# One group of half-tile checks moved behind five row checks, and three weight loads moved behind two row loads, in a Fourier-mixing and one-token FFN kernel

## The chip, the core and the metric

The kernel runs on one core of one Trainium2 chip. The metric is the device time of one execution in microseconds. Three timed runs of the kernel before gave 203.41, 270.83 and 200.82 us; their median is 203.41 us. The execution that was profiled took 201.27 us.

A core has five engines that run side by side, each with its own instruction stream in fixed order: TensorE (PE, matrix products), VectorE (DVE), ScalarE (ACT), GpSimd (POOL) and SyncE (SP). An instruction that waits holds up everything behind it on its engine. Transfers between device memory and the on-chip buffer are issued by SP (ordinary loads, called direct) and by POOL (loads by a table of row numbers, called gathers); all of them share 16 DMA engines.

## The reference

The input `x` is 2048 tokens by 576 columns. The kernel computes a Fourier mixing layer with a residual, then a feed-forward network that runs for a single token:

```python
a = einsum("bsd,ed->bse", LN(x), dft_hid_re)          # 576 x 576
b = einsum("bsd,ed->bse", LN(x), dft_hid_im)
h = x + einsum("ts,bse->bte", dft_seq_re, a) - einsum("ts,bse->bte", dft_seq_im, b)   # 2048 x 2048
z = LN(h)
r = z @ w_r                                           # one score per token
t = argmax(r)                                         # C = 1: one token
y = (silu(z[t] @ w_gate) * (z[t] @ w_up)) @ w_down    # 576 -> 4608 -> 576
out = h + z;  out[t] += sigmoid(r[t]) * y
```

All data is float32. The four Fourier matrices and the three weight matrices come as inputs, and their bytes are most of what is read: 72.86 MB read and 6.49 MB written by the page.

## The kernel before

**What is computed quickly, and what is checked.** The sequence matrices are really cosines and sines, so one half of them is a mirror image of the other. The kernel multiplies with a quarter of each matrix only (lines 556 to 568) and, beside that, loads the rest as well and checks that it is the mirror image. The checks write differences (or sums) to a buffer `Q` on DVE; ACT squares `Q` and sums the squares (line 368). If the sum over all checks is not tiny at the end, a slow general path under `tc.If` computes everything anew (from line 1331). In the runs here it is not taken.

**How the sequence matrices are tiled.** There are 16 blocks of rows, `j` = 0 to 15, each for the cosine (`i` = 0) and the sine (`i` = 1). Blocks `j` and `16 - j` mirror each other. Group 0 of `GROUPS` is the blocks 1 to 5, called group one in the heading of this change; group 1 is 6, 7, 0, 8. For a group, the five (or four) block tiles of 128 x 1152 floats stay in a buffer `D` while PE multiplies with them: `D0` holds the cosine of the first group, `D1` its sine. These ten tiles are loaded by `c_first(0, 0)` and `c_first(0, 1)`, ahead of everything else of the matrices.

**The two kinds of check.**

- A half check (`off_h`, line 382): for tiles that PE uses, the second half of the 128 columns must mirror the first. It reads the tiles in `D` alone and needs no further load. One call is two DVE instructions (line 387).
- A row check (`c_check`, line 833): for block `j` it loads the mirrored part of `j` (a gather on POOL), block `16 - j` (a direct load on SP) and the mirrored part of `16 - j` (another gather); three DVE instructions compare them: line 375 twice (`off_s`) and line 380 once (`off_t`).

The loads of a row check go to a ring of buffers: seven called `R`, and those of the tiles in `D` that are free at the time. A load can be issued only when the checks that read its buffer before have run. In the first group the row check of block 1 uses `R` 0 to 2, that of block 2 `R` 3 to 5, that of block 3 `R` 6 and two tiles of `D2`; block 4 takes the other two tiles of `D2` and then `R` 0, block 5 `R` 2, 1 and 3. The first direct loads of the sine's row checks go to `R` 4 (freed by block 2) and `R` 2 (freed by the first instruction of block 5's cosine check); behind these two, in SP's order, stand the four tiles of the second group's cosine.

**The buffer Q** has two slots, taken in turn. A check that takes a slot waits for the square of the check that had it before.

**The weights W** of the hidden transform (`wt`, three tiles, four direct loads, lines 403 and 405) are needed by ACT (line 415) and then by PE (line 610), when all five products with the sequence matrix of the first group are done (`seq`, line 565) and written to `Z` by DVE (line 583).

**The order of the work.** The kernel is not written in order of time. A planner (`Plan`) gets every step with its engine, an estimated duration and what it depends on, and arranges the steps of each engine by a list schedule. The steps of SP and POOL that load are chained in the order in which the code makes them; on DVE and ACT the planner chooses among the steps that are ready. The order that comes out is fixed in the program: it is not changed at run time.

**What follows** the two groups: residual and row statistics on DVE and ACT, the choice of the token, and the feed-forward network, whose 31.9 MB of weights (three matrices of 576 x 4608 floats) are loaded into every buffer that comes free (lines 1173 to 1181) and multiplied on DVE, POOL and ACT; PE adds up the last product (line 1228), DVE finishes the token's row (line 1241), and it is stored.

Of the kernel before, what the change touches and what calls it, by code (L numbers as in the profile page):

```python
# [14 lines left out]
P = 128  # L15
# [22 lines left out]
GROUPS = [[1, 2, 3, 4, 5], [6, 7, 0, 8]]  # L38
# [5 lines left out]
HALVES = [[(0, 2), (2, 2), (4, 1)], [(0, 2), (2, 2)]]  # L44
# [8 lines left out]
HM = P // 2  # L53
# [17 lines left out]
class Plan:  # L71
# [6 lines left out]
    def add(self, eng, dur, fn, *deps, tail=0.0, push=0.0):  # L78
        flat = []
        for d in deps:  # L80
            flat += d if isinstance(d, list) else [d]
        n = {"eng": eng, "dur": dur, "fn": fn, "deps": [d for d in flat if d], "tail": tail, "push": push}
        n["i"] = len(self.ops)
        self.ops.append(n)
        return n
# [57 lines left out]
def kernel(  # L143
# [172 lines left out]
    Q = QT.bitcast(BF16).rearrange("p (n w) -> p n w", n=2)  # L316
# [62 lines left out]
        o = Q[:, u % 2, 14 * P : QW].rearrange("p (k m) -> p k m", m=P)  # L379
        dve.tensor_tensor(o, C[NK - j, i, False], C[j, i, False][:, :, ::-1], op=SIGN[i])  # L380

    def off_h(g, c, n, i, u):

        o = Q[:, u % 2, i * 9 * n * HM : (i + 1) * 9 * n * HM].rearrange("p (c k m) -> p c k m", k=9, m=HM)
        t = DT[g, i][:, c : c + n]
        for k, op in enumerate((OP.subtract, OP.add)):
            dve.tensor_tensor(o[:, :, k::2, :], t[:, :, k::2, 0:HM], t[:, :, k::2, HM:P], op=op)  # L387
# [296 lines left out]
    add = plan.add  # L684

    def then(f, *args):
        return lambda: f(*args)
# [8 lines left out]
    def load(eng, f, mb, *deps):  # L696

        ns = in_flight[eng]
        n = add(eng, 0.1 if eng == "SP" else 1.3, f, *deps, ns[-8:-7])
        d = add("DMA", mb / 0.405, None, n, moved[-1:])  # L700
        moved.append(d)
        ns.append(add("COME", 0.0, None, d, tail=1.8))
        return n, ns[-1]
# [4 lines left out]
    def in_turn(eng, f, mb, *deps):  # L708
        LAST[eng], d = load(eng, f, mb, LAST[eng], *deps)
        return d  # L710

    IDENT = []
    for k, n in X_LOADS:
        d = in_turn("SP" if k < 9 else "POOL", then(load_x, k, n), 0.295 * n)
# [11 lines left out]
    for a, b in X_RUNS:  # L726
# [4 lines left out]
        m = [add("ACT", 0.95, then(measure, k), f, push=push) for k, f in zip(ks, r)]  # L731
        o = add("POOL", 0.3, then(totals, a, b), e, m)
# [3 lines left out]
        o = add("POOL", 2.0, then(biases, a, b), r, o)  # L736
# [6 lines left out]
    users = {b: [] for b in ["XF", "Z", "Q", "WA", "WB", "WC", *range(N_RAW)]}  # L743
# [16 lines left out]
    for k in FOLDED:  # L760
        dg, use, at = [], [], []
        for sl in slots_of(k):
            n = next(places)
            UF[sl] = LATER[n]
            at.append(PLACE[n])
            if k in PAIRS:
                u, w = dgs.take()
# [34 lines left out]
    CU = {}  # L802

    def c_load(j, i, mirror):
        CU[j, i, mirror] = ring("POOL" if mirror else "SP", load_c, 0.46 if mirror else 0.59, j, i, mirror)
# [8 lines left out]
            LAST["SP"], d = load("SP", then(load_c, None, j, i, False), 0.59, w, LAST["SP"])  # L814
            CU[j, i, False] = u, d

    def c_half(g, c, m):
        u, w = qs.take()
        cus = [[CU[j, i, False] for j in GROUPS[g][c : c + m]] for i in range(2)]
        n = [  # L820
            add("DVE", 0.16 + 0.62 * m, then(off_h, g, c, m, i, u), [d for _, d in cus[i]], w)
            for i in range(2)
        ]
        for i in range(2):
            for b, _ in cus[i]:
                users[b].append(n[i])
        squares(u, 9 * m * P, n)

    def squares(u, w, n, ps=P):
        SQUARES.append(add("ACT", 0.3 + w / 1200, then(square, u, w, ps), n))  # L830
        qs.users[u].append(SQUARES[-1])

    def c_check(j, i):

        u, w = qs.take()
        u0, d0 = CU[j, i, False]
        c_load(j, i, True)
        u1, d1 = CU[j, i, True]
        n = [add("DVE", 1.08, then(off_s, j, i, u, 0), d0, d1, w)]
        users[u0] += n  # L840
        users[u1] += n
        free.append(u1)
        if j in PAIRS:
            m = NK - j
            c_load(m, i, False)
            c_load(m, i, True)
            (u2, d2), (u3, d3) = CU[m, i, False], CU[m, i, True]
            n.append(add("DVE", 1.08, then(off_s, m, i, u, 1), d2, d3, w))
            users[u3].append(n[1])
            n.append(add("DVE", 1.36, then(off_t, j, i, u), d0, d2, w))  # L850
            users[u0].append(n[2])
            users[u2] += n[1:]
            free.extend([u3, u2])
        if u0[0] == "D1":
            free.append(u0)
        squares(u, QW if j in PAIRS else 7 * P, n)
# [3 lines left out]
    def w_first():  # L860
        for n in range(3):
            LAST["SP"], d = load(
                "SP", then(load_w, None, n), (0.59, 0.59, 0.22)[n], LAST["SP"], users["W" + "ABC"[n]]
            )
            WL.append(d)
# [19 lines left out]
    def seq_step(g, n):  # L885
        nonlocal pe_last
        w = len(GROUPS[g]) * HM
        (z0, w0_), (z1, w1_) = zs.take(), zs.take()
        need = [CU[j, i, False][1] for i in PARTS[n] for j in GROUPS[g]]
        pe_last = add("PE", 9 * w * 0.00171, then(seq, g, n), need, FOLDS, w0_, w1_, pe_last)  # L890
        for i in PARTS[n]:
            for c in range(len(GROUPS[g])):
                users[D_TAG[g, i], c].append(pe_last)
        users["XF"] = [pe_last]
        SEQ[g, n] = pe_last, z0, z1

    def keep_step(g, n):
        w = len(GROUPS[g]) * HM
        pe, z0, z1 = SEQ[g, n]
        u, wo = odds.take()  # L900
        h = add("ACT", 0.11 + 0.00085 * w, then(keep, g, n, 0), pe, wo)
        l = add("DVE", 2 * (0.07 + 0.00106 * w), then(keep, g, n, 1), h, ZU.get((g - 1, n > 0), []))
        odds.users[u].append(l)
        zs.users[z0].append(l)
        zs.users[z1].append(h)
        KEPT.setdefault(g, []).append(l)
# [44 lines left out]
        for b in [b for b in free if type(b) is tuple and b[0] == tag]:  # L951
            free.remove(b)

    for c, m in HALVES[0]:
        c_half(0, c, m)
    for j in GROUPS[0][:3]:
        c_check(j, 0)
    w_first()
    for j in GROUPS[0][3:]:
        c_check(j, 0)  # L960
    for n in (0, 1, 4, 2, 3):
        seq_step(0, n)
        keep_step(0, n)
# [18 lines left out]
    for i in range(2):  # L982
        for j in GROUPS[1]:
            c_check(j, i)
    for c, m in HALVES[1]:
        c_half(1, c, m)
    for c in range(2):
        hid_step(0, c)
    for n in (0, 1):
# [133 lines left out]
    o = add("DVE", 1.0, check_sum, SCORES, SQUARES, xs_is)  # L1123
    o = add("PE", 0.3, check_all, o)
# [6 lines left out]
    for b in range(NJ // TW):  # L1131
        j = TW * b
# [198 lines left out]
    with tc.If(T["mv"], preferred_fallthrough_block=False):  # L1331
        with ExitStack() as gen:
# [33 lines left out]
            with ExitStack() as hs:  # L1366
# [9 lines left out]
                with tc.For_i(0, NK, 1) as k:  # L1376
                    dve.tensor_copy(xr, row_of(GX, k))
                    norm(xn, xr, "x")
                    for a in range(5):
                        w = min(P, D - a * P)  # L1380
# [4 lines left out]
                    for c in range(4):  # L1385
                        pa = zbank(f"gpa{c}")
                        for a in range(5):
                            w = min(P, D - a * P)
# [115 lines left out]
```

## Time and profile before

| what | value |
|---|---|
| timed runs | 200.82, 203.41, 270.83 us (median 203.41) |
| profiled execution | 201.27 us, span from first to last instruction 199.2 us |
| busy: PE, DVE, ACT, POOL | 65%, 83%, 71%, 62% of the span |
| DMA | 77.81 MB moved, 391 GB/s over the span |

The page cuts the span into 40 slices of 5 us and gives, for each, how busy every engine was in tenths, and how many GB/s the DMA engines moved. Other views list the instructions of one engine in order of time; a row there gives start, duration, engine, line, operation, what is written and read, a count, and in brackets how long the engine had stood idle before it and what released it. Rows of `SPq` are the moments at which SP issues loads; a time there is the issue, not the transfer. A view of stretches gives the DMA's share and rate for any piece of time.

### The profile page before, as it was taken

How to read it: one execution, taken by the hardware profiler on the slowest of the kernel's cores; microseconds unless marked ns; L12 is line 12 of the kernel's file. 1: busy time of each engine (PE TensorE's matmuls, PEld its weight loads, DVE VectorE, ACT ScalarE, POOL GpSimd, SP SyncE). 2: the span in 40 equal slices, each digit the busy share in tenths (PEclk: the TensorE clock that was granted, in tenths of full speed). 3: DMA queues.
4: the chain of work that ended last, by engine and by line, in shares of the span. 5: the costliest groups of instructions: out<-in, count | busy, mean ns of one | idle time of the engine just before them, and what ended most of it. 6: DMA issues, size and time to landing. Idle time of an engine off the chain costs nothing. (4 is left out here: it accounts for less than half of the span.)

```text
span 199.2 us, 2787 instructions
## 1 busy us (share of the span) xinstructions
PE 130.4 (65%) x758; PEld 89.9 (45%) x758; DVE 166.1 (83%) x419; ACT 140.5 (71%) x259; POOL 122.8 (62%) x134
## 2 busy tenths in 40 slices
PE   0007989999999989899999996600241444085840
PEld 0005667764767778677877774400121111043220
DVE  4389997989999859997999999999839997899410
ACT  2298863783987794799587599997629999786400
POOL 6578888495528878998870000006439999998500
PEclk9999999999999999999999999985555555555798
DMA  5999999999979999999999999999999999999991
GB/s 190 361 418 415 411 411 409 409 372 346 402 275 366 415 398 391 404 407 412 407 401 418 420 420 422 427 414 423 422 428 425 428 422 420 431 420 412 422 387 42
DMA packets 14491, 77.81 MB, mean 391 GB/s; under 512 B 1855, under 2 KB 1859, under 8 KB 11143
## 3 DMA queue, kind: packets, MB, share of 16 engines
q1 hardware_dynamic: 10463, 56.56, 70.8%
q0 software_dynamic: 4000, 21.03, 26.3%
q8 instruction: 7, 0.11, 0.2%
q14 instruction: 13, 0.11, 0.1%
q10 hardware_dynamic: 8, 0.00, 0.0%
HBM read 72.86 MB, written 6.49 MB: 398 GB/s over the span
## 5 line engine op out<-in xcount | busy, mean ns | idle before, releaser
L368 ACT ACTIVATE Q<-Q 128x2944 bf16<-128x2944 bf16 (+5 forms) x26 | 55.4, 2133 | 19.9 <-DVE Q L375 7.0
L610 PE MATMUL py<-W,Z 128*128 128x289 f32 x180 | 45.3, 408 | 2.3 <-DVE X L619 2.3
L565 PE MATMUL ps<-D,XF 128*128 128x320 f32 (+3 forms) x216 | 45.0, 408 | 1.2 <-DMA D<-in_ct_dram 0.8
L301 POOL DMA_INDIRECT R<-in_ct_dram,ic x21 | 34.1, 1625 | 14.5 <-DVE Q L375 10.5
L610 PEld LDWEIGHTS py<-W,Z 128*128 128x128 f32 x180 | 33.7, 189 | 13.6 <-issue 2.9
L565 PEld LDWEIGHTS ps<-D,XF 128*128 128x128 f32 (+1 forms) x216 | 32.1, 172 | 13.8 <-issue 2.5
L1201 POOL TENSOR_TENSOR D<-D,Z 128x1152 f32<-128x1152 f32 x8 | 20.8, 2618 | 1.2 <-SPq L1331 1.2
L667 POOL DMA_DIRECT2D out_dram<-X x1 | 0.6, 606 | 30.0 <-ACT X L661 30.0
L301 POOL DMA_INDIRECT D<-in_ct_dram,ic x11 | 16.1, 1468 | 3.4 <-issue 2.4
L498 ACT ACTIVATE junk<-X,XT 128x576 bf16<-128x576 f32 x16 | 12.4, 772 | 8.0 <-DVE W L459 6.5
L1206 ACT ACTIVATE junk<-D 128x576 bf16<-128x576 f32 x20 | 13.7, 683 | 4.0 <-POOLq L1331 2.3
L1228 PE MATMUL pd<-XF,H 128*1 128x144 f32 x80 | 5.3, 440 | 16.1 <-DVE H L1220 13.3
L537 PE MATMUL fo<-W,diag 128*128 128x288 f32 (+1 forms) x8 | 3.9, 665 | 16.4 <-DVE diag L528 16.4
L387 DVE TENSOR_TENSOR Q<-D 128x640 bf16<-128x640 f32 (+3 forms) x20 | 12.7, 691 | 1.4 <-DMA D<-in_ct_dram 1.4
L380 DVE TENSOR_TENSOR Q<-R,D 128x1152 bf16<-128x1152 f32 x10 | 13.4, 1349 | 0.0
L630 ACT ACTIVATE junk<-X,TD 128x576 bf16<-128x576 f32 x16 | 12.3, 768 | 1.5 <-DVE X L619 1.3
L375 DVE TENSOR_TENSOR Q<-R,D 128x896 bf16<-128x896 f32 x11 | 11.9, 1083 | 1.3 <-DMA D<-in_ct_dram 1.2
L661 ACT ACTIVATE X<-X,BB,UP 128x576 f32<-128x576 f32 x14 | 10.8, 855 | 2.4 <-DVE BB L642 2.4
L623 DVE SCALAR_TENSOR_TENSOR junk<-X,wr 128x576 bf16<-128x576 f32 x16 | 12.1, 754 | 0.3
L375 DVE TENSOR_TENSOR Q<-D 128x896 bf16<-128x896 f32 x11 | 11.8, 1081 | 0.0
L619 DVE SCALAR_TENSOR_TENSOR X<-py,X 128x576 f32<-128x576 f32 x16 | 11.5, 748 | 0.0
L375 DVE TENSOR_TENSOR Q<-R 128x896 bf16<-128x896 f32 x10 | 10.8, 1084 | 0.7 <-DMA R<-in_ct_dram,ic 0.7
(202 smaller groups left out, 262.5 us busy)
## 6 DMA issues: line engine op xcount, KB each, us to landing
D<-in_ct_dram SPq DMA_DIRECT2D x22, 576.0 KB
R<-in_ct_dram SPq DMA_DIRECT2D x10, 576.0 KB
D<-in_wu_dram SPq DMA_DIRECT2D x5, 1152.0 KB
D<-in_wd_dram SPq DMA_DIRECT2D x4, 1152.0 KB
R<-in_wg_dram SPq DMA_DIRECT2D x3, 1152.0 KB
D<-in_wg_dram SPq DMA_DIRECT2D x3, 1152.0 KB
out_dram<-X SPq DMA_DIRECT2D x2, 1440.0 KB
X<-in_x_dram SPq DMA_DIRECT2D x4, 576.0 KB
```

What stands on the lines that cost most here:

```text
L301: pool.indirect_dma_start(tile, None, view, bass.IndirectOffsetOnAxis(ap=rows, axis=0), element_offset=at)
L368: act.activation(t, t, AF.Square, accum_out=DS[0 : t.shape[0], n : n + 1])
L375: dve.tensor_tensor(o, C[j, i, True][:, 0:7, :], C[j, i, False][:, 7:0:-1, :], op=SIGN[i])
L380: dve.tensor_tensor(o, C[NK - j, i, False], C[j, i, False][:, :, ::-1], op=SIGN[i])
L387: dve.tensor_tensor(o[:, :, k::2, :], t[:, :, k::2, 0:HM], t[:, :, k::2, HM:P], op=op)
L498: act.activation(junk[:, 0:D], X[:, k, 0:D], AF.Square, bias=XT[:, n : n + 1], scale=-float(D), accum_out=VX[:, n : n + 1],)
L565: pe.matmul(cm(ZP[g, n][k % 2][p0 : p0 + m], w), XF[:, q, m0 : m0 + m], DT[g, i][:, :, k, 0:HM], start=k in (0, 1), stop=k in (6, 7),)
L610: pe.matmul(YP[GROUPS[g][c]][:, h, 0:w], Z[:, a, c * P : (c + 1) * P], w_block(a)[:, h * HD : h * HD + w], start=(a == 0), stop=(a == 4),)
L623: dve.scalar_tensor_tensor(junk2, X[:, k, 0:D], 1.0, wr, op0=OP.mult, op1=OP.mult, accum_out=TD[:, n, 0:1])
L630: act.activation(junk[:, 0:D], X[:, k, 0:D], AF.Square, bias=TD[:, n, 1:2], scale=-float(D), accum_out=VAR[:, n : n + 1],)
L1201: pool.tensor_tensor(t, t, xs.unsqueeze(1).to_broadcast([P, JW, D]), op=OP.mult)
L1206: act.activation(junk[:, 0:D], WB[w, j][:, r, :], AF.Copy, accum_out=acc[:, j + r : j + r + 1])
```

## The change

`c_half` took one part of a group's tiles and compared its cosine and its sine together, one slot of `Q` for both. `halves` takes a list of parts and a list of cosine and sine. For the first group the cosine's halves of all five tiles now share one slot and stay where they were; the sine's halves share another slot and are made behind the five cosine row checks. The three tiles of W are loaded behind the loads of the fifth row check instead of behind those of the third. The second group is treated as before.

```diff
-    def off_h(g, c, n, i, u):
-
-        o = Q[:, u % 2, i * 9 * n * HM : (i + 1) * 9 * n * HM].rearrange("p (c k m) -> p c k m", k=9, m=HM)
+    def off_h(g, c, n, i, u, at):
+
+        o = Q[:, u % 2, at : at + 9 * n * HM].rearrange("p (c k m) -> p c k m", k=9, m=HM)
...
-    def c_half(g, c, m):
+    def halves(g, parts, ms):
         u, w = qs.take()
-        cus = [[CU[j, i, False] for j in GROUPS[g][c : c + m]] for i in range(2)]
-        n = [
-            add("DVE", 0.16 + 0.62 * m, then(off_h, g, c, m, i, u), [d for _, d in cus[i]], w)
-            for i in range(2)
-        ]
-        for i in range(2):
-            for b, _ in cus[i]:
-                users[b].append(n[i])
-        squares(u, 9 * m * P, n)
+        n, at = [], 0
+        for i in ms:
+            for c, m in parts:
+                cus = [CU[j, i, False] for j in GROUPS[g][c : c + m]]
+                o = add("DVE", 0.16 + 0.62 * m, then(off_h, g, c, m, i, u, at), [d for _, d in cus], w)
+                for b, _ in cus:
+                    users[b].append(o)
+                n.append(o)
+                at += 9 * m * HM
+        squares(u, at, n)
...
-    for c, m in HALVES[0]:
-        c_half(0, c, m)
+    halves(0, HALVES[0], [0])
     for j in GROUPS[0][:3]:
         c_check(j, 0)
-    w_first()
     for j in GROUPS[0][3:]:
         c_check(j, 0)
+    w_first()
+    halves(0, HALVES[0], [1])
...
-    for c, m in HALVES[1]:
-        c_half(1, c, m)
+    for part in HALVES[1]:
+        halves(1, [part], [0, 1])
```

What the planner makes of it. SP, the direct loads behind those of the ten tiles, before:

```order
L357 DMA R<-in_ct_dram 128x1152 x2
L357 DMA D<-in_ct_dram 128x1152
L403 DMA W<-in_wt_dram 128x2x576 x2
L403 DMA W<-in_wt_dram 33x2x576
L405 DMA W<-in_wt_dram 32x576
L357 DMA D<-in_ct_dram 128x1152
L357 DMA R<-in_ct_dram 128x1152 x3
L357 DMA D<-in_ct_dram 128x1152 x5
```

and now:

```order
L357 DMA R<-in_ct_dram 128x1152 x2
L357 DMA D<-in_ct_dram 128x1152 x2
L357 DMA R<-in_ct_dram 128x1152
L403 DMA W<-in_wt_dram 128x2x576 x2
L403 DMA W<-in_wt_dram 33x2x576
L405 DMA W<-in_wt_dram 32x576
L357 DMA R<-in_ct_dram 128x1152 x2
L357 DMA D<-in_ct_dram 128x1152 x5
```

The loads of blocks 12 (`D`) and 11 (`R`) have moved ahead of the four loads of W; all else on SP stands as before, and POOL's order is the same throughout.

DVE at the start of the checks, from the last fold of the input on, before (half checks of two parts, the first row check, half checks of the last two parts; the two parts ahead of these rows are the cosine and the sine of tiles 3 and 4):

```order
L548 TENSOR_SCALAR XF<-fo_370 128x287
L387 TENSOR_TENSOR Q<-D 128x2x5x64
L387 TENSOR_TENSOR Q<-D 128x2x4x64
L387 TENSOR_TENSOR Q<-D 128x2x5x64
L387 TENSOR_TENSOR Q<-D 128x2x4x64
L375 TENSOR_TENSOR Q<-R,D 128x896
L375 TENSOR_TENSOR Q<-R 128x896
L380 TENSOR_TENSOR Q<-R,D 128x1152
L387 TENSOR_TENSOR Q<-D 128x5x64
L387 TENSOR_TENSOR Q<-D 128x4x64
L387 TENSOR_TENSOR Q<-D 128x5x64
L387 TENSOR_TENSOR Q<-D 128x4x64
```

and now, at the same place:

```order
L548 TENSOR_SCALAR XF<-fo_370 128x287
L375 TENSOR_TENSOR Q<-R,D 128x896
L387 TENSOR_TENSOR Q<-D 128x5x64
L387 TENSOR_TENSOR Q<-D 128x4x64
L375 TENSOR_TENSOR Q<-R 128x896
L380 TENSOR_TENSOR Q<-R,D 128x1152
L724 TENSOR_SCALAR bt<-tf 128x16
L375 TENSOR_TENSOR Q<-R,D 128x896
L380 TENSOR_TENSOR Q<-R,D 128x1152
L375 TENSOR_TENSOR Q<-R 128x896
```

The first row check now begins behind two parts of the half checks (both cosine) instead of four, with the third cosine part inside it, and the second row check follows at once.

DVE at the end of the cosine's row checks, now (`ps_2` and `ps_3` are products of the sequence matrix):

```order
L380 TENSOR_TENSOR Q<-R,D 128x1152
L583 SCALAR_TENSOR_TENSOR Z<-ps_2_0_466,os_2_491 128x5x64 x2
L387 TENSOR_TENSOR Q<-D 128x2x5x64
L387 TENSOR_TENSOR Q<-D 128x2x4x64
L387 TENSOR_TENSOR Q<-D 128x2x5x64
L387 TENSOR_TENSOR Q<-D 128x2x4x64
L387 TENSOR_TENSOR Q<-D 128x5x64
L387 TENSOR_TENSOR Q<-D 128x4x64
L583 SCALAR_TENSOR_TENSOR Z<-ps_3_0_494,os_3_523 128x5x64 x2
```

The six instructions of the sine's half checks stand between the last two products; the next row below is the first row check of the sine, as before.

## The prediction

> **What bounds the kernel now.** I read the page's slices first, then stretches of time around the one slice that stands out, then the rows of SP, POOL and DVE at that place. The slices of 5 us:
>
> ```profile
> DMA  5999999999979999999999999999999999999991
> GB/s 190 361 418 415 411 411 409 409 372 346 402 275 366 415 398 391 404 407 412 407 401 418 420 420 422 427 414 423 422 428 425 428 422 420 431 420 412 422 387 42
> ```
>
> The DMA engines are busy in nine tenths or more of every slice between the first and the last, with one exception: slice 11, from 55 to 60 us. No other engine is so full for so long. So the time is the time that the bytes need, plus what the DMA loses. Cut finer (columns: stretch, its length, busy us of PE, PEld, DVE, ACT, POOL, granted clock, DMA share, GB/s):
>
> ```profile
> 56.00:57.00 1.00, 1.00 (x5) 0.68 (x5) 1.00 (x2) 0.79 (x1) 0.00 (x0) 1.00 0.89 363
> 57.00:58.00 1.00, 1.00 (x6) 0.68 (x5) 1.00 (x2) 1.00 (x1) 0.00 (x0) 1.00 0.22 86
> 58.00:59.00 1.00, 1.00 (x5) 0.50 (x4) 1.00 (x2) 1.00 (x3) 0.61 (x1) 1.00 0.87 205
> 59.00:60.00 1.00, 1.00 (x5) 0.56 (x4) 1.00 (x3) 0.80 (x2) 1.00 (x1) 1.00 0.95 341
> 60.00:61.00 1.00, 1.00 (x5) 0.78 (x5) 1.00 (x4) 1.00 (x1) 0.70 (x2) 1.00 1.02 392
> 61.00:62.00 1.00, 1.00 (x6) 0.78 (x5) 1.00 (x2) 1.00 (x1) 0.70 (x2) 1.00 0.97 359
> ...
> 59.00:193.00 134.00, 88.74 (x590) 62.11 (x592) 116.11 (x279) 101.76 (x190) 83.01 (x53) 0.80 1.01 414
> ```
>
> From 57 to 59 us only 86 and 205 KB per us (the same as GB/s) move, against 414 over the long stretch behind it. Why nothing is there to move is in SP's and POOL's rows:
>
> ```profile
> 30.71 2.35 SPq L403 DMA_DIRECT2D W<-in_wt_dram  x3
> 33.63 0.34 SPq L405 DMA_DIRECT2D W<-in_wt_dram  x1
> ...
> 41.47 0.33 SPq L357 DMA_DIRECT2D R<-in_ct_dram  x1
> ...
> 57.14 0.33 SPq L357 DMA_DIRECT2D R<-in_ct_dram  x1
> ...
> 57.52 2.78 SPq L357 DMA_DIRECT2D D<-in_ct_dram  x5
> ...
> SPq L357 <- DVE Q L375: 29.1, 9, 7.1
> ```
>
> ```profile
> 11.01 1.06 POOL L301 DMA_INDIRECT R<-in_ct_dram,ic  x1 [0.16 <-issue]
> ...
> 35.67 1.39 POOL L301 DMA_INDIRECT D<-in_ct_dram,ic  x1 [0.30 <-issue]
> 39.45 4.29 POOL L301 DMA_INDIRECT R<-in_ct_dram,ic  x1 [2.39 <-DVE Q L375]
> ...
> 58.39 1.82 POOL L301 DMA_INDIRECT R<-in_ct_dram,ic  x1 [4.25 <-DVE Q L375]
> ```
>
> SP's load at 57.14 and POOL's gather at 58.39 both waited for row checks on DVE (line 375), SP 29.1 us in nine waits over the whole run. And DVE is the engine that was late:
>
> ```profile
> 33.71 1.43 DVE L387 TENSOR_TENSOR Q<-D 128x640 bf16<-128x640 f32 x2 [1.36 <-DMA D<-in_ct_dram]
> ...
> 35.42 2.75 DVE L387 TENSOR_TENSOR Q<-D 128x640 bf16<-128x640 f32 x4
> 38.09 1.08 DVE L375 TENSOR_TENSOR Q<-R,D 128x896 bf16<-128x896 f32 x1
> ...
> 41.37 1.56 DVE L387 TENSOR_TENSOR Q<-D 128x320 bf16<-128x320 f32 x4
> ...
> 44.32 1.36 DVE L380 TENSOR_TENSOR Q<-D 128x1152 bf16<-128x1152 f32 x1 [0.52 <-ACT Q L368]
> ...
> 52.84 1.00 DVE L583 SCALAR_TENSOR_TENSOR Z<-ps,sgn,os 128x320 f32<-128x320 f32 x2
> ...
> 56.03 1.09 DVE L375 TENSOR_TENSOR Q<-R,D 128x896 bf16<-128x896 f32 x1
> ...
> 60.90 1.08 DVE L375 TENSOR_TENSOR Q<-R,D 128x896 bf16<-128x896 f32 x1
> ```
>
> The row at 56.03 is the first instruction of block 5's check; it ends at 57.12 and SP issues into the buffer it read at 57.14. The row at 60.90 is the sine's first row check.
>
> **The change part by part.** *The sine's half checks leave.* Ahead of the end of block 5's first instruction go: the pair at 33.71 (1.43), half of the four at 35.42 (1.38), half of the four at 41.37 (0.78), together 3.59 us; the wait of 1.36 for the sine tiles, which the pair had; the wait of 0.52 for a slot of `Q`, since two fewer slots are taken; and the `Z` write of 1.00 at 52.84, which now stands behind. 57.12 - 3.59 - 1.36 - 0.52 - 1.00 = 50.65. What comes instead is waiting for data. DVE would now be at the second instruction of the first row check at 33.71 - 1.36 + 1.71 (the pair and a fold, 33.71 to 35.42) + 1.08 + 0.78 = 35.9; before, it got there at 38.09 + 1.08 = 39.2 and found its data. So the new wait there lies between 0 and 3.3. The second row check needs the slot of the cosine's halves squared, one square nearly as wide as this row:
>
> ```profile
> L368 ACT ACTIVATE Q<-Q 128x2944 bf16<-128x2944 bf16 x14 | 37.2, 2654 | 14.4 <-DVE Q L375 7.0 <-DVE Q L380 6.4 <-issue 1.0
> ```
>
> 35.9 + 2.65 + some 0.2 for reading the sum is 38.8, against 35.9 + 1.08 + 1.36 = 38.3 for the end of the first row check: 0.5 us at most, and nothing if DVE has waited for data. So block 5's first instruction ends between 50.7 and 54.5. I take 53, since the gather at 39.45 also took 4.29 us and its data (block 12) may be waited for once more. The load of 57.14 is then issued at about 53, the four `D` tiles behind it by 56. POOL's order is unchanged; its gather of 58.39 hangs on block 5's second instruction and comes as much earlier.
>
> *The gap.* The buffers ran dry at 57.0 and the load of 57.14 brought a full flow only near 58.4, so the load must be issued by 55.7 to leave no gap. Even 54.5 does. What is won from 57 to 59 is 2 - (86 + 205) / 414 = 1.30 us. The slow start behind it, 59 to 62, lost 3 - (341 + 392 + 359) / 414 = 0.36 us; I count 0.2 of it.
>
> *The loads of W leave their place.* At 30.71 to 33.97 SP no longer issues 1.40 MB (two loads of 576 KB, one of 148.5, one of 72), and the two row loads behind take their place; W now waits behind the load of block 11, which waits for block 1's check. Could the DMA run dry before that?
>
> ```profile
> 0.00:40.00 40.00, 22.66 (x82) 16.33 (x83) 31.20 (x116) 24.53 (x51) 29.26 (x76) 1.00 0.97 378
> ```
>
> By 40 us 378 x 40 = 15.12 MB have moved. Issued without W, block 11 and later gathers are 4.72 MB of `x`, 14 loads of 0.59 MB and, from 11.01 to 35.67, seven gathers of 0.459 MB (128 x 896 floats): 16.19 MB. The rest lasts until 40 + 1.07 / 0.414 = 42.6. Block 11's load goes out when the first row check ends, between 38.3 and 41.6, and W right behind: no gap, or 0.3 us at the late end. The gather of 39.45 comes earlier on top.
>
> W's first reader is on ACT:
>
> ```profile
> 55.07 0.39 ACT L415 ACTIVATE W<-W 128x2 f32<-128x2 f32 x3
> ```
>
> Ahead of W's end stand 16.19 MB, block 11, W and about five gathers: 20.5 MB, that is 40 + 5.4 / 0.39 = 53.8 (0.39 as a rate between the slices of 402 and 372). It is just in time; 1 or 2 us late would hold ACT's next square and copy, for which DVE has the sine's half checks to do. Nothing is counted.
>
> *The sine's half checks arrive.* 3.59 us of DVE work stand ahead of the last `Z` write and of 60.90. DVE's work up to there is the same, so it gets there at 60.90 - 1.36 - 0.52 + (0 to 3.3) = 59.0 to 62.3: 1.4 us late at worst. Behind it DVE has waits for DMA data:
>
> ```profile
> 67.20 1.09 DVE L375 TENSOR_TENSOR Q<-R 128x896 bf16<-128x896 f32 x1 [0.68 <-DMA R<-in_ct_dram,ic]
> ...
> 74.85 0.76 DVE L422 TENSOR_TENSOR Q<-D,W 128x576 bf16<-128x576 f32 x1 [2.38 <-ACT Q L368]
> ```
>
> (The second I take for a gather of W that came late: ACT had squared what stood in its slot by then.) Both waits shrink with gathers issued earlier, so a late microsecond is given back. ACT saves one square, off the path; no instruction is added on any engine.
>
> *The end.* The chain that ended last is
>
> ```profile
> 192.24 1.20 PE pd L1228 x32
> ...
> 193.47 0.37 DVE orow L1241
> ...
> 192.24 1.16 PE L1228 MATMUL pd<-W,H 128*1 128x144 f32 x32 [0.94 <-SPq L1331]
> ```
>
> PE had waited 0.94 us before its last group, which reads the tile of W that SP's last loads fill, so an earlier DMA ends the run earlier. Sum: -1.30 - 0.2 = -1.5, hence 201.27 - 1.5 = 199.8 us. The three timed runs have their median at 203.41 and their fastest at 200.82; the profiled one is near the fastest, and I forecast on its scale.
>
> The Trainium skill ("DMA: Bandwidth & Descriptors", Where 436 GB/s comes from) gives some 358 GB/s as the most that one core gets from device memory. By that the gap would be worth 1.19 us and the slow start nothing, so 200.1. The rows above, 414 GB/s over 134 us, do not agree, and they decide.
>
> **The rivals.** *The gap only moves: 201.3.* In
>
> ```profile
> 91.00:104.00 13.00, 13.00 (x71) 10.41 (x71) 11.81 (x19) 9.52 (x11) 10.56 (x9) 1.00 1.01 404
> ```
>
> DVE is busy 11.81 of 13 us and releases the buffers; if it is not earlier there, a DMA that is 1.5 us ahead runs dry and the gain is lost. For it: that share, 0.91. Against it: the waits of 0.68 and 2.38 that DVE can lose.
>
> *More comes back: 198.7.* The stretch in which W moves is slow though the DMA is busy:
>
> ```profile
> 43.00:48.00 5.00, 5.00 (x37) 2.50 (x36) 4.48 (x7) 2.76 (x5) 2.73 (x3) 1.00 1.05 319
> ```
>
> 5 x (1 - 319 / 414) = 1.15 us. If W, with gathers beside it, moves at the full rate now, that is won too. Against it: W's small loads are the same.
>
> *Slower, 203.8: POOL's gathers stretch.* Some gathers take 4.3 us in place of about 1, three in a row here:
>
> ```profile
> 78.86 4.43 POOL L301 DMA_INDIRECT R<-in_ct_dram,ic  x1 [0.30 <-issue]
> 83.60 4.33 POOL L301 DMA_INDIRECT D<-in_ct_dram,ic  x1 [0.30 <-issue]
> 88.23 4.32 POOL L301 DMA_INDIRECT R<-in_ct_dram,ic  x1 [0.30 <-issue]
> ```
>
> DVE now runs its checks without the pauses of 1.36 and 0.52, and if that is what stretches them, the gathers of blocks 12, 5 and 11 start at 37.4 and end at 37.4 + 3 x 4.63 - 0.3 = 51.0. The gather of 58.39 ended at 60.21 and was read at 67.20 after a wait: 7 us. Block 11's data would be there at 58, where DVE wants it at 54, and all behind it is 4 us late: 199.8 + 4 = 203.8. It makes the run slower from 1.5 us on, that is from three in a row. The Trainium skill ("SBUF — State Buffer", Who interferes with whom) has a rule that could do this: a DVE instruction with two inputs in the buffer shuts out a GpSimd instruction that reads it, for its whole length; it infers, though, that making descriptors is not among what is shut out. The trace leaves it open: beside a full DVE the gather of 58.39 took 1.82, that of 39.45 took 4.29.
>
> **How the numbers follow.** The forecast gets 0.50, the moved gap 0.22, more back 0.18, slower 0.07, the rest 0.03. The range takes in 198.7 to 201.3, with 0.7 below and 1.5 above for the scatter of the timed runs around the profiled one (200.82 and 203.41): 198.0 to 202.8. 2%, about what a measurement here can tell, is 4.0 us: faster by that would need more than everything lost between 40 and 62, 0.05; slower, four stretched gathers in a row, 0.04; within, 0.91.
>
> **What would show it.** The load of 57.14 at 52 to 55; slice 11 at about 400 GB/s; no POOL wait of 4.25; the half checks of the sine near 57 to 61; the row of 74.85 without its wait; the last PE group about 1.5 us earlier. It is wrong if a slice between 35 and 45 or behind 60 falls instead, or if block 11's or 12's check waits more than 3 us for its gather.

## The result: 1% slower

The changed kernel took 203.53 us (median; 201.42 to 205.05), the kernel before 201.41 us in the same session. The ratio is 1.01, 95% interval 1.008 to 1.012: slower by 2.1 us, where 199.8 us was forecast, a gain of 1.5. One percent is little, but the interval lies above 1, and 203.53 lies above the forecast's range of 198.0 to 202.8. (Times are medians of all executions; ratios leave out those that stand far above the fastest of their kernel: four of the changed kernel's 22, and one or two of seven to eleven in five of the versions below.)

The profiled execution of the changed kernel took 203.47 us, with a span of 201.4 us (before: 201.27 and 199.2). Its slices of 5 us:

```profile
DMA  5999999999999999999978999999999999999991
GB/s 188 357 422 413 409 415 407 411 407 397 333 383 411 394 399 403 411 408 413 403 217 299 422 428 425 426 421 412 425 423 431 397 398 390 423 432 417 412 416 56
```

The slice of 55 to 60 us is mended (383 in place of 275). Two others have fallen, 100.7 to 110.8 us: 217 and 299. Stretches of the two traces show the balance (columns: stretch, its length, busy us of PE, PEld, DVE, ACT, POOL, granted clock, DMA share, GB/s). Before:

```profile
40.00:63.00 23.00, 22.55 (x101) 14.27 (x100) 22.41 (x31) 17.94 (x25) 13.93 (x9) 1.00 0.97 352
63.00:100.00 37.00, 35.72 (x153) 28.62 (x153) 32.75 (x53) 27.56 (x35) 32.12 (x17) 1.00 1.02 402
100.00:112.00 12.00, 12.00 (x71) 8.61 (x70) 12.00 (x22) 8.68 (x17) 3.70 (x4) 1.00 1.01 409
112.00:190.00 78.00, 35.11 (x294) 20.57 (x292) 67.36 (x200) 61.75 (x133) 43.79 (x31) 0.65 1.01 423
```

And after:

```profile
40.00:63.00 23.00, 23.00 (x104) 14.80 (x104) 22.26 (x30) 18.36 (x22) 17.10 (x10) 1.00 1.02 384
63.00:100.00 37.00, 33.09 (x142) 26.37 (x141) 26.99 (x45) 24.56 (x34) 19.04 (x15) 1.00 1.02 405
100.00:112.00 12.00, 10.50 (x64) 7.42 (x63) 12.00 (x19) 9.21 (x13) 4.14 (x3) 1.00 0.83 280
112.00:190.00 78.00, 36.72 (x277) 22.65 (x277) 70.73 (x202) 61.96 (x135) 42.13 (x31) 0.67 1.01 418
```

Each difference in rate, times the length and divided by 414 GB/s, is time: 1.8 us won from 40 to 63, 0.3 won to 100, 3.7 lost from 100 to 112, 0.9 lost behind it. The sum, 2.6 lost, stands for the 2.2 by which the span grew. Notice DVE between 63 and 100 us: it is busy 27.0 us instead of 32.8, with the DMA at full rate all the time. Most of the difference is one wait for data (8.46 us, below), while data came in as fast as ever.

The rows around the old gap did what the prediction said. SP, POOL, DVE and ACT after (columns: start, duration, engine, line, operation, out<-in, count, and in brackets the wait before it and what ended it):

```profile
43.16 9.01 SPq L357 DMA_DIRECT2D R<-in_ct_dram  x2
52.23 4.67 SPq L357 DMA_DIRECT2D D<-in_ct_dram  x5
...
53.94 1.89 POOL L301 DMA_INDIRECT R<-in_ct_dram,ic  x1 [0.30 <-DVE Z L583]
...
50.74 1.08 DVE L375 TENSOR_TENSOR Q<-R,D 128x896 bf16<-128x896 f32 x1
...
55.73 3.49 DVE L387 TENSOR_TENSOR Q<-D 128x640 bf16<-128x640 f32 x6
...
60.76 1.08 DVE L375 TENSOR_TENSOR Q<-R,D 128x896 bf16<-128x896 f32 x1
...
56.76 0.21 ACT L415 ACTIVATE W<-W 128x2 f32<-128x2 f32 x1 [0.87 <-DMA W<-in_wt_dram]
```

The load that waited for block 5's check until 57.14 is the second of the pair at 43.16, issued as that check's first instruction ends at 51.8. The six half checks of the sine stand at 55.73, and the sine's first row check comes at 60.76 (before: 60.90). The new gap has one wait behind it:

```profile
89.89 1.08 DVE L375 TENSOR_TENSOR Q<-R,D 128x896 bf16<-128x896 f32 x1
99.43 1.09 DVE L375 TENSOR_TENSOR Q<-R,D 128x896 bf16<-128x896 f32 x1 [8.46 <-DMA D<-in_ct_dram]
...
72.24 7.68 SPq L357 DMA_DIRECT2D D<-in_ct_dram  x5
80.79 10.53 SPq L357 DMA_DIRECT2D R<-in_ct_dram  x3
105.75 0.33 SPq L1174 DMA_DIRECT2D R<-in_wg_dram  x1
...
90.82 0.96 POOL L301 DMA_INDIRECT D<-in_ct_dram,ic  x1 [0.30 <-issue]
100.79 1.82 POOL L301 DMA_INDIRECT R<-in_ct_dram,ic  x1 [9.00 <-DVE Q L375]
```

DVE stands for 8.46 us, until 99.43, for the rows of block 10, a plain load by SP. It is the last of the five loads at 72.24 to 79.92: the four sine tiles of group two stand ahead of it. While DVE stands, no buffer comes free; SP issues nothing from 91.3 to 105.75, POOL nothing from 91.8 to 100.79, and when what had been issued is used up, the DMA runs dry. Before, the same check had waited 1.19 us:

```profile
92.32 1.07 DVE L375 TENSOR_TENSOR Q<-R,D 128x896 bf16<-128x896 f32 x1
94.58 1.09 DVE L375 TENSOR_TENSOR Q<-R,D 128x896 bf16<-128x896 f32 x1 [1.19 <-DMA D<-in_ct_dram]
...
76.30 7.00 SPq L357 DMA_DIRECT2D D<-in_ct_dram  x5
```

There the load went out as the last of five at 76.30 to 83.30, that is 3.4 us later than after, and DVE had it 4.9 us earlier. What the two queues moved between its issue and its landing (columns: queue and kind, packets, MB, share of the 16 engines' time), before, 83 to 94 us:

```profile
q1 hardware_dynamic: 699, 2.85, 64.9%
q0 software_dynamic: 294, 1.63, 36.7%
```

and after, 80 to 99 us:

```profile
q0 software_dynamic: 793, 4.55, 59.0%
q1 hardware_dynamic: 790, 3.22, 42.9%
```

q1 is SP's queue (plain loads), q0 is POOL's (gathers). After, as many packets went from the one as from the other, 790 and 793, as if both had work all the time. A gather's packets are larger (4.55 MB / 793 = 5.7 KB on the mean, against 4.1 KB), so SP's loads moved at 3.22 / 19 = 169 GB/s. Before, POOL's queue sent only 294 packets beside 699, and SP's loads moved at 2.85 / 11 = 259 GB/s. At that rate the 3.22 MB would have taken 12.4 us in place of 19 (an estimate from these two counts): most of the wait of 8.46 us. The Trainium skill ("DMA: Bandwidth & Descriptors", Queues, rings and completion order) says that each DMA engine takes its queues in turn, a packet from each. The counts agree with that.

POOL's queue was fuller because the gathers were issued earlier. Here are the first and the fourteenth gather, counted from the first of W on, before:

```profile
60.51 0.94 POOL L301 DMA_INDIRECT R<-in_wt_dram,iw  x1 [0.30 <-DVE Z L583]
...
92.86 1.36 POOL L301 DMA_INDIRECT R<-in_ct_dram,ic  x1 [0.31 <-issue]
```

and after:

```profile
56.13 3.90 POOL L301 DMA_INDIRECT R<-in_wt_dram,iw  x1 [0.30 <-DVE Z L583]
...
84.16 0.95 POOL L301 DMA_INDIRECT R<-in_ct_dram,ic  x1 [0.30 <-issue]
```

The lead is 4.4 us at the first and 8.7 at the fourteenth.

So the theory to be tested: the change lets POOL's gathers run ahead; gathers that lie in their queue take more than half of the DMA; SP's plain loads then come late, and one of them is what DVE or PE needs next.

### The profile page after: what moved, and what is told of

The parts are those of the page before. It is cut to its first block, busy times and chain, and to the rows that moved or that the text cites. A ratio compares the mean times of both kernels' runs of the same rounds, so it can differ in the third digit from the quotient of the medians.

```text
span 201.4 us, 2785 instructions
## 1 busy us (share of the span) xinstructions
PE 130.4 (65%) x758; PEld 90.2 (45%) x758; DVE 166.4 (83%) x419; ACT 140.1 (70%) x257; POOL 114.5 (57%) x134
## 5 line engine op out<-in xcount | busy, mean ns | idle before, releaser
L301 POOL DMA_INDIRECT R<-in_ct_dram,ic x21 | 30.4, 1449 | 19.8 <-DVE Q L375 16.7
L301 POOL DMA_INDIRECT D<-in_ct_dram,ic x11 | 13.9, 1265 | 6.9 <-DMA R<-in_ct_dram,ic 3.2
```

The costliest lines, as they stand in the source:

```text
L301: pool.indirect_dma_start(tile, None, view, bass.IndirectOffsetOnAxis(ap=rows, axis=0), element_offset=at)
```

## The experiments

Ratios are to the kernel before, with 95% intervals; the runs of one session share its runs of before. "The theory" is the one above.

### The two parts apart

The loads of W alone (the half checks go back ahead of the row checks):

```diff
-    halves(0, HALVES[0], [0])
+    for part in HALVES[0]:
+        halves(0, [part], [0, 1])
     for j in GROUPS[0][:3]:
...
     w_first()
-    halves(0, HALVES[0], [1])
```

> Only the loads of W are moved; the sine's half checks stand ahead of the row checks as before the change. Theory (the loss comes from DVE waiting 8.46 us at 99.43 us for the plain load of block 10, which stands in SP's queue behind the four sine tiles of group two and gets too small a share beside gathers that run ahead): here DVE is not earlier at its row checks, so POOL does not run ahead and that wait stays near the 1.19 us it had before; the gap at 57 to 59 us stays; 201 to 202 us. Rival (the W loads in their new place are what costs: the gathers around them are late): 203 us or more.

Measured: 200.96 us, ratio 1.0014 (0.9988 to 1.0041). DVE's wait for block 10 is as before the change, and so is the old gap, though its loss now lies in two slices (320 and 309, from 49 to 59 us):

```profile
GB/s 189 379 420 410 412 416 407 410 399 395 320 309 411 412 395 395 401 408 414 412 405 423 414 421 429 423 425 410 423 427 426 423 430 425 423 417 417 418 399 40
...
94.56 1.09 DVE L375 TENSOR_TENSOR Q<-R,D 128x896 bf16<-128x896 f32 x1 [1.04 <-DMA D<-in_ct_dram]
...
q1 hardware_dynamic: 706, 2.88, 65.5%
q0 software_dynamic: 293, 1.63, 36.5%
```

The last two rows are the queues from 83 to 94 us, and they are those of the kernel before (699 and 294). This also answers a question that the trace before leaves open: was POOL's queue short there only because three gathers took more than 4 us, at 78.86, 83.60 and 88.23? In this trace only the third did (4.32 us, at 88.36), and the counts are the same.

The half checks alone (the loads of W go back behind the third row check):

```diff
     halves(0, HALVES[0], [0])
     for j in GROUPS[0][:3]:
         c_check(j, 0)
+    w_first()
     for j in GROUPS[0][3:]:
         c_check(j, 0)
-    w_first()
     halves(0, HALVES[0], [1])
```

> Only the sine's half checks are moved; the loads of W stay where they were before the change. Theory: the row checks and POOL's gathers run ahead as in the changed kernel, DVE waits 5 us or more for block 10's load near 95 to 100 us, the gap at 57 to 59 us is gone and a new one stands near 100 to 109 us: 202.5 to 204 us. Rival (the W loads cost it): 199.5 to 200.5 us.

Measured: 203.35 us, ratio 1.0126 (1.0095 to 1.0158). It is the half checks that cost, as the theory has it, but the place was another: the old gap is not gone, it is worse.

```profile
GB/s 189 358 418 414 411 412 410 410 392 348 390 99 405 418 381 400 409 407 411 401 402 388 412 424 426 426 419 419 421 428 422 424 428 430 421 419 420 416 416 65
...
54.85 1.36 DVE L380 TENSOR_TENSOR Q<-D 128x1152 bf16<-128x1152 f32 x1 [6.69 <-DMA D<-in_ct_dram]
```

At 48 us DVE meets block 12's rows, a plain load that stands behind W's 1.40 MB, and waits 6.69 us for it. Again the DMA is busy until it runs dry at 55 us. With the checks drawn forward, W in its old place makes the next plain load late; the changed kernel moved W away and met the same kind of wait at 91 us. This run does not show the sharing between the queues: its late load stands behind W in SP's own queue, and its wait for block 10 is only 0.75 us.

### The late load drawn forward, and the gathers held late

Block 10's load alone is put ahead of the four sine tiles in SP's queue, in the finished order of the planner, so that nothing else moves (`BY`, filled where the loads are planned, holds them by block):

```diff
...
-    for n in plan_ffn(best[1])[1]:
+    todo = plan_ffn(best[1])[1]
+    early, first = BY[10, 0], BY[6, 1]
+    todo.remove(early)
+    todo.insert(todo.index(first), early)
+    for n in todo:
```

> The changed kernel, with one SP load put elsewhere: block 10's, which stood behind the four sine tiles of group two, now stands ahead of them; the order on every engine is otherwise the same. Theory: the load is issued near 68 us in place of 79.53 and is there when DVE wants it at 91 us, so the wait of 8.46 us goes; DVE's next wait is for block 9's load (issued at 80.79, landed near 100), at most 6 us; the gather of 100.79 goes out near 92; the gap of 100 to 109 us shrinks from 3.7 us lost to 1 us or less: 200 to 201.5 us. Rival (the gap is only where a slower end of the run, POOL's products or the stores, shows first): 203 to 204 us, no gain although the wait goes.

Measured: 203.18 us, ratio 1.0107 (1.0065 to 1.0149). The wait for block 10 went, the time did not. The profiled execution (204.49 us, at the slow end of its six, 201.62 to 204.60) shows what took its place there:

```profile
GB/s 194 369 418 414 411 409 409 416 400 399 351 383 413 378 414 398 411 409 335 286 376 353 293 399 432 419 430 413 403 433 427 418 426 428 424 428 413 408 404 34
...
75.94 10.94 PE L565 MATMUL ps<-D,XF 128*128 128x256 f32 x36 [6.41 <-DMA D<-in_ct_dram]
...
83.04 0.38 ACT L579 ACTIVATE os<-ps 128x256 f32<-128x256 f32 x1 [6.76 <-PE ps L565]
...
85.83 1.09 DVE L375 TENSOR_TENSOR Q<-R,D 128x896 bf16<-128x896 f32 x1 [3.57 <-ACT Q L368]
...
97.10 2.08 DVE L375 TENSOR_TENSOR Q<-R,D 128x896 bf16<-128x896 f32 x2
```

The pair at 97.10 holds block 10's check, without a wait. But another plain load came late: PE waited 6.41 us for group two's first tiles (issued by SP from 52.22 on; 2.19 us in the changed kernel's trace), ACT stood behind PE with its copy of the sums, and DVE behind ACT for a slot of `Q`. The time is lost where the DMA then runs short, 91 to 116 us (five slices of 286 to 376), and not at the end of the run, as the rival had it. Up to 66 us the two programs give every engine the same instructions in the same order, yet the tiles came 4 us later. POOL's rows of the two traces differ before that, the changed kernel's first:

```profile
48.82 4.82 POOL L301 DMA_INDIRECT R<-in_ct_dram,ic  x1 [1.25 <-DVE Q L375]
```

and this run's:

```profile
48.81 1.55 POOL L301 DMA_INDIRECT R<-in_ct_dram,ic  x1 [1.46 <-DVE Q L375]
```

The same gather took 3.3 us less here, so the gathers behind it came earlier: from 54 to 56 us POOL's queue moved 0.45 MB beside the loads of SP, and nothing in the changed kernel's trace. The other traces with both parts of the change in which SP brings these tiles fit: with 4.82 or 4.83 us for this gather PE waits 2.3 us at most (five traces), with 1.55 us it waits 6.41 and 5.83 (this one and the next). So which of SP's loads is the late one went with the length of one gather; why that length differs is not known.

Next, POOL is held up behind three gathers of group two's cosine, where the trace before shows stretched ones:

```diff
     gather(t[:, 0:7, :], ...)
+    if i == 0 and j in (7, 9, 10):
+        for _ in range(38):
+            pool.memset(held, 0.0)
```

> The changed kernel, with POOL held up by some 3.4 us (38 small memsets of 0.09 us) behind each of the gathers of blocks 10, 7 and 9 of group two's cosine, about what three stretched gathers took there before the change (4.43, 4.33 and 4.32 us in place of about 1); nothing else. Theory: fewer gathered bytes stand beside SP's loads between 78 and 92 us, block 10's load lands earlier than 99.4 us, DVE's wait of 8.46 us shrinks to 5 us or less, and the run is not slower, 202 to 203.5 us, although POOL does 10 us more. Rival (late gathers are what costs): the 10 us turn up as waits of DVE for gathers, 205 us or more.

Measured: 203.06 us, ratio 1.0114 (1.0074 to 1.0154). The memsets took 5.5 us each time, not 3.4, so POOL did 16.5 us more, and the run is not slower than the changed kernel: POOL's time in itself is not what costs. Nor did it help. Here too PE waited for group two's first tiles (the first hold-up begins at 75.05 us, when that wait was all but over), and the DMA ran short from 91 to 101 us (209 and 264 GB/s). The last hold-up lies there, but the run before dips there without one, so how much of the dip is the hold-up's is not shown.

```profile
GB/s 189 351 421 409 416 406 408 414 404 403 343 400 414 379 408 406 411 407 209 264 338 373 417 421 425 426 421 419 418 428 421 425 426 430 416 430 415 419 424 101
...
75.44 10.68 PE L568 MATMUL ps<-D,XF 128*128 128x256 f32 x36 [5.83 <-DMA D<-in_ct_dram]
...
89.31 5.52 POOL L358 MEMSET held<- 1x1 f32 x38
```

### Holding the gathers once, earlier

If gathers that run ahead are the cause, the place for the hold-up is where they begin to: behind the last gather of W.

```diff
     gather(t if n < 5 else t[0:33, :], wt, ...)
+    if n == 5:
+        for _ in range(38):
+            pool.memset(held, 0.0)
```

> The changed kernel with one hold-up on POOL: 38 small memsets (5.5 us in the run before) behind the last gather of W, ahead of the gather of block 3's sine, where before the change a gather of W took 5.58 us; nothing else. Theory (gathers that run ahead take more than half of the DMA, so SP's plain loads, of which one or another is the next thing that DVE or PE needs, come late): SP's loads of 52 to 58 us, the first tiles of group two, get nearly all of the DMA for some 5 us and land before PE wants them, the waits of 3 to 9 us on DVE between 80 and 100 us go or halve, no slice between 60 and 115 us falls under 370 GB/s, 199.5 to 201.5 us. Rival (gathers that come later are only later): the 5.5 us turn up as a wait of DVE for a gather near 67 to 80 us, 204 us or more.

Measured: 200.43 us, ratio 0.9951 (0.9927 to 0.9975). With 5.5 us of work on POOL that computes nothing, the changed kernel is 3 us faster than without, and a little faster than before.

```profile
GB/s 188 342 422 413 410 414 404 412 406 405 352 361 411 409 382 401 409 412 409 406 385 333 430 426 428 423 421 411 428 425 424 400 403 393 428 423 426 411 417 51
...
63.13 5.51 POOL L411 MEMSET held<- 1x1 f32 x38
...
96.83 1.09 DVE L375 TENSOR_TENSOR Q<-R,D 128x896 bf16<-128x896 f32 x1 [5.57 <-DMA D<-in_ct_dram]
```

The slices of the new gap are 385 and 333 in place of 217 and 299. The expectation was right in the time and too good in the detail: DVE still waits 5.57 us for block 10, and one slice is under 370. Nor did group two's first tiles come earlier: PE waits 2.28 us for them, and 2.19 in the changed kernel's trace. What the hold-up won is seen behind it. From 70 to 84 us SP's queue moved 2.91 MB in place of 2.35, about one load of 0.59 MB more, and the wait for block 10 is 2.9 us shorter, as much as the two profiled executions differ by (203.47 and 200.58 us).

With block 10's load drawn forward as well, by the two edits above together:

> The changed kernel with the hold-up of POOL and with block 10's load ahead of the four sine tiles. With the hold-up alone DVE still waited 5.57 us for that load, at 96.83, and one slice stood at 333 GB/s. Theory: that wait goes, no slice between 60 and 190 us is under 380 GB/s, 199.3 to 200.3 us. Rival (the wait's length no longer sets anything): 200.3 to 201 us.

Measured: 199.39 us, ratio 0.9929 (0.9896 to 0.9962). The wait for block 10 is gone, and DVE's longest wait is now 3.10 us, at 99.22, for another plain load. From 59 us on no slice but the last is under 380; the row below is the stretch of the former gap:

```profile
GB/s 187 359 417 413 411 413 410 414 403 404 350 372 407 413 383 398 408 412 410 407 407 415 421 425 421 425 425 413 417 433 428 390 412 414 427 429 415 410 400 28
...
100.00:112.00 12.00, 12.00 (x72) 8.81 (x71) 12.00 (x22) 8.90 (x18) 0.00 (x0) 1.00 1.02 413
```

So drawing the load forward won nothing in the run whose trace has PE waiting 6.41 us for group two's first tiles, and 1.0 us (200.43 to 199.39) beside the hold-up, where that wait is 1.99 us. The intervals of the two versions with the hold-up overlap, so this 1.0 us is not sure.

### Plain loads in POOL's own queue

The same cause from another side: put plain loads among the gathers, in one queue, in the order of need.

```diff
+    on = pool if b is None and (g, i) == (1, 1) else sp
-    sp.dma_start(t, ct[j, :, i, 0:9, :])
+    on.dma_start(t, ct[j, :, i, 0:9, :])
```

Group two's sine tiles by POOL:

> The changed kernel, with the four plain loads of group two's sine tiles issued by POOL, in POOL's queue, in place of SP's; nothing else. Theory: the loads that DVE needs next (blocks 10 and 9) no longer stand behind 2.36 MB in SP's queue, block 10's is issued near 68 us and there by 85, DVE's wait for it goes; the gathers behind the four loads come later, and POOL is held by the four buffers until they are free. The first tiles of group two still come by SP, and where the run has PE waiting for them near 72 to 82 us (as in the run with one load first) that loss stays: 200.5 to 203 us. Rival (late gathers are what costs): 204 us or more.

Measured: 200.36 us, ratio 0.9959 (0.9925 to 0.9993). Block 10's load goes out at 66.64, DVE's wait at that check is 2.38 us (the profile names nothing that ended it), and the gap is gone (410 and 419 from 99 to 109 us):

```profile
GB/s 192 384 421 414 413 410 407 414 404 401 349 376 409 410 365 402 407 414 409 410 410 419 420 424 422 426 419 413 426 428 426 420 430 422 419 422 418 422 292 26
...
66.64 0.38 SPq L358 DMA_DIRECT2D D<-in_ct_dram  x1
```

The cosine tiles by POOL, `(g, i) == (1, 0)`:

> The changed kernel, with the four plain loads of group two's cosine tiles (SP's of 52 to 58 us) issued by POOL, in POOL's queue; nothing else. Theory: they come in POOL's order, ahead of the gathers of W, and land before 70 us, so PE has no wait of 2 to 6 us for them at 71 to 76 us and ACT none of 6 us behind PE; the rows of blocks 13 to 11 in SP's queue come earlier too. POOL waits for the four buffers until 57 us, which holds the gathers behind by some 4 us. 200 to 202.5 us. Rival: the gathers so held are the ones that DVE needs near 60 us (block 14's sine), 204 us or more.

Measured: 200.47 us, ratio 0.9975 (0.9944 to 1.0005). PE's wait at 71 to 76 us went. In its place DVE waited 2.97 us for a gather, until 69.81, and the slices of 90 to 100 us are at 285 and 346.

Both by POOL, `g == 1`:

> The changed kernel, with both sets of four plain loads of group two's tiles issued by POOL. Theory: both sources of late plain loads go, 199.5 to 202 us, and no DVE wait for a plain load over 2 us between 60 and 110 us. Rival (late gathers are what costs): 204 us or more.

Measured: 201.14 us, ratio 0.9968 (0.9940 to 0.9995); no better than either alone. Between 60 and 110 us the profile shows no wait of DVE for a plain load any more, but waits for gathers: 2.88 us until 69.12, and 1.65 until 111.23. So plain loads ahead of gathers in one queue can make the gathers late in their turn; that this is why the run gains no more is likely, not shown.

Sine tiles by POOL, with half the hold-up (19 memsets):

> The changed kernel with the sine tiles of group two in POOL's queue and half the hold-up (19 memsets, 2.75 us) behind the last gather of W. With the sine tiles in POOL's queue alone PE waited 2.08 us for group two's first tiles and no slice from 60 to 190 us was under 409 GB/s, but the slices of 50 to 60 were at 349 and 376. Theory: the hold-up protects the first tiles in those executions in which they come late; the median falls a little or stays, 199.8 to 200.5 us. Rival (2.75 us of POOL are on the path now): 201.5 us or more.

Measured: 199.52 us, ratio 0.9905 (0.9881 to 0.9928). Two of its seven executions, the profiled one among them, took some 204.9 us; in the profiled one two gathers on POOL took 7.03 and 8.39 us (at 61.49 and 80.49), the DMA ran short from 81 to 91 us (126 and 215 GB/s), and DVE waited 6.99 us at block 10's check. With such executions this version's gain is not secure.

### Is it the change, or would any kernel gain?

The same remedies on the kernel before the change. First the hold-up:

> The kernel before the change, with the same hold-up of POOL (38 small memsets) behind the last gather of W. Theory: here DVE is late and POOL's gathers do not run ahead of SP's loads, so there is nothing to win; the gathers of block 3's and 4's sine go out 5.5 us later, near 75 and 78 us, and DVE wants them at 79 to 85 and finds them late by 0 to 4 us: 201 to 204 us. Rival (held gathers make any version of this kernel faster): 200.2 us or less.

Measured: 202.99 us, ratio 1.0068 (1.0031 to 1.0104): slower, as the theory has it. The DMA has less to do from 76 to 81 us (227 GB/s in that slice), and DVE finds a gather late by 0.94 us, at 82.98. Then the sine tiles by POOL:

> The kernel before the change, with the four plain loads of group two's sine tiles issued by POOL, in its queue. Theory: the wait of DVE for block 10's load is 1.19 us here and the gap of 57 to 59 us stays, so there is little to win: 200.5 to 201.7 us. Rival (this queue is better by itself): 200 us or less.

Measured: 202.42 us, ratio 1.0094 (1.0048 to 1.0140). The expectation was no more than 201.7; it is slower than that, and the rival, a gain, is further off still. The same edit wins 3.2 us behind the change (203.53 to 200.36) and loses 1 to 2 us without it (1.1 by the medians, 1.9 by the ratio). What is mended is something that the change brings.

## Why the prediction was wrong

**What held.** The old gap came from late row checks, and it closed: the waiting load went out at 51.84 (forecast: 50.7 to 54.5, taken 53), POOL's wait of 4.25 us went, 57 to 59 us moved at 410 and 417 GB/s. The DMA did not run dry from 35 to 50 us (slices 411, 407, 397). The sine's first row check came at 60.76 (forecast 59.0 to 62.3), and the waits of 0.68 and 2.38 us behind it are gone. W came later than reckoned: its last reader started at 56.76, where the sum had W's end at 53.8. ACT's next square was held as feared, and it cost DVE only 0.74 us, as the half checks stood there. W's slow stretch stayed slow in its new place (slice 10 at 333), so the rival "more comes back" fell. The last PE group came at 194.81, 2.6 us later than before, not 1.5 us earlier. And the sign of being wrong that the prediction had named came: two slices behind 60 us fell, to 217 and 299.

**The step that failed** is the one under "the sine's half checks arrive": "Both waits shrink with gathers issued earlier, so a late microsecond is given back." Earlier gathers were booked as pure gain, and what the DMA loses behind 62 us was put at nothing. It measured 3.7 us from 100 to 112, and 0.9 behind that nothing here explains. For the 3.7, the gathers that lay in their queue took DMA from SP's plain loads (169 GB/s for these in place of 259), and DVE stood 8.46 us for one of them. The sum reckoned with one DMA, in which bytes move in the order of issue ("ahead of W's end stand 16.19 MB, block 11, W and about five gathers"). There are two queues, which sent 790 and 793 packets side by side, and nothing in the sum said which of the two would bring the next thing needed. W's end, some 3 us late, is in part the same error: by 53.8 us 20.52 MB had moved, as reckoned, but 2.92 MB of what moved behind 40 us were gathers, over six of them for the five of the sum. Beside that the flow was slow, 300 GB/s from 52 to 56 us; how the 3 us divide between the two is not known.

**The rivals.** "The gap only moves" had the place nearly right (91 to 104 us; DVE stood from 91 to 99, the DMA ran short from 101 to 111), and both the reason and the size wrong. It had the DMA run dry because DVE, full of work, would not be earlier there. DVE was earlier, 89.89 in place of 92.32 at group two's first row check, and then stood for data. So the loss was not bounded by the gain it took back: 3.7 us, not 1.5. The rival that was slower had the time nearly right (203.8) by a mechanism that did not come: it had POOL's gathers stretched, and in truth they ran ahead. What the Trainium skill ("SBUF — State Buffer", Who interferes with whom) infers, that a DVE instruction with two inputs in the buffer does not shut out the making of descriptors, is not settled by the trace after: eight gathers from 62 to 76 us, beside DVE at work, took 0.94 to 1.93 us each, but those at 48.82 and 56.13 took 4.82 and 3.90, beside DVE instructions of that kind too. In the trace before, three long gathers in a row (4.43, 4.33 and 4.32 us, from 78.86 on) left more of the DMA to SP's queue: from 88 to 94 us it sent 457 packets and POOL's 108. Three such in a row did not occur after. That their absence costs the time is not borne out: with the loads of W alone two of the three are missing and nothing is lost, and hold-ups put in by hand in that place won nothing. The hold-up that won stood some 12 us earlier.

**Runs against the theory.** Its figure held the time of seven of the twelve experiments. Three more came out a little better than it (200.96 for 201, 200.36 for 200.5, 199.52 for 199.8). Two missed: the one load drawn forward won nothing where 2 to 3 us were foreseen, since the theory had picked one late load and there was another, and the kernel before with the sine tiles by POOL lost 1 us or more where little was foreseen. In the half checks alone the time was right and the place wrong: the old gap, some 45 us ahead of where it was looked for, with the same kind of wait. The rival "gathers that come later only cost" held in the kernel before. In the changed kernel it held nowhere in the time, though with the cosine tiles by POOL DVE did wait up to 2.97 us for gathers.

**What stays open.** Why like gathers take 0.94 us in one place and 3.4 to 8.39 in another, and the gather at 48.8 us 1.55 us in one execution and 4.82 in another, was not tried. Nor was the loss of 0.9 us behind 112 us followed (slices of 397, 398 and 390): the hold-up run has the same three (400, 403, 393), and the two parts apart do not.

## What to carry to other kernels

In these traces two DMA queues that both had work sent as many packets each, whatever was needed first; so ask of an edit that lets one queue run ahead what is due next in the other, and how long its bytes take at the share that is left. A gap in the DMA can be the second half of a story, as here: look some microseconds before it for an engine that stands for one late load while the DMA is full. Two remedies to try are loads issued in the order of need in one queue, and a hold on the queue that runs ahead; both won here behind the change and lost without it.

## What was not expected of the hardware

The share itself: with both queues full, 790 packets of SP's loads against 793 of gathers in 19 us, 169 against 4.55 / 19 = 239 GB/s, from 80 to 99 us. That 5.5 us of useless work on POOL makes the changed kernel 3 us faster. And that executions can differ in which load is late: PE's wait for group two's first tiles was 2.19, 6.41 and 5.83 us in three traces whose programs are the same up to 66 us, and a gather on POOL had taken 4.82, 1.55 and 1.55 us ahead of it.
